# The last 224 rows of w_out as one row a lane: fewer pieces in the MLP, other DMA engines

## The chip, the cores and the metric

The kernel runs on one core of a Trainium2 chip. Its time is the device time of one execution in microseconds (us). The engines are PE (matrix products), DVE (VectorE), ACT (ScalarE), POOL (GpSimd) and SP, which here only issues transfers. The core's transfers run on sixteen DMA engines.

## What is computed

One decoding step for four sequences: the sum of the input, of attention with a key and value cache, and of a gated MLP, both on the normalised input.

```python
B, Sq, D = 4, 1, 640;  H = 32 heads, Sk = 4096 cached keys, Dh = 128;  F = 1728, Fh = 864
xn = layernorm(x)
q = xn @ wq                                        # 640 x 4096
p = softmax(q . k_cache * Dh ** -0.5)              # for each sequence and head
att = (p . v_cache) @ wo                           # 4096 x 640
z = gelu(xn @ w_in)                                # 640 x 1728, tanh form
g = w_sp * layernorm(z[Fh:]) + b_sp                # w_sp and b_sp are single numbers
out = x + att + (z[:Fh] * g) @ w_out               # 864 x 640
```

All tensors are bf16. The two caches have 134 MB each and are read once; the other weights together are some 14 MB.

## The kernel before

The attention is cut into 16 units, `NU`: a group of 8 heads (`HG` = 4 groups) of one sequence. A unit's keys are 8 MB, laid with 256 keys a lane on 128 lanes, in four tiles of 64 keys a lane; they live in seven places of `k_ring`. A unit's values are 8 MB and fill `v_all`. For each key tile DVE multiplies by the broadcast query (`product`, L537) and adds the halves (`fold_half`, L543), and PE sums the rest with identity products into PSUM (`sums`, L555). DVE then takes row sums (L569), the maximum (L578 to L588), ACT the exponentials (L596), DVE lays them out by head in `p_m` (L607), and PE multiplies by the values (`weighted`, L631). A group of four units ends with a projection by `wo` (L699).

The order on PE, DVE, ACT and SP is written out by hand: the loop over `NK * NU` = 64 key tiles at the end of the function. Transfers stand in the list `loads`; `pump()` issues from it on SP's queue, in order, as long as the places of the next entry are free. Each DMA also takes one of eight completion semaphores in turn and waits until that one's last user has landed.

At the start v_all isn't needed for values yet, so `wq`, `w_in` and most of `w_out` are put there. The 864 rows of `w_out` are cut by `W_OUT` into parts (lanes, rows a lane, transfers): 128 lanes of 5 rows in `v_all`; 128 lanes of 1 row in `p_m`; and 12 lanes of 8 rows in `p_m`, loaded as four transfers of every fourth lane, so of 3 lanes each with 8 rows of 640 bf16 (10240 bytes) a lane. The last part is `load_w_few`, behind the second half of unit 0's keys:

```python
loads = [k_load(0, 0, 1), k_load(0, 1, 2), (load_w, []), k_load(0, 2, 4), (load_w_few, []), k_load(1)]
```

The number of rows a lane over all parts, `NFC` = 5 + 1 + 8 = 14, is the number of pieces in which the MLP runs: `gmlp()` makes 2 x 14 x 5 products with `w_in` (L404), element steps on tiles of 128 x (2 x 14 x 4) (L414 to L432, L488 to L500) and 14 x 2 products with `w_out` (L503). It runs in steps between the first key tiles. The first values can be loaded when L503 is done with `v_all` (`busy.remove(V)`).

The input `x` (4 rows) is one transfer on ACT's queue (L101); the two single numbers `w_sp` and `b_sp` are loaded on the same queue just before the loop (L735, L736) and cast on POOL (L464, L466). The query path is x, its statistics and normalisation (L265 to L274), its transposition (L289, L294), and q (L303), which needs `wq`.

The end of the kernel is the last unit's values in falling sizes, the last part of `wo` in six transfers, the last projection (L699), one copy on ACT (L823) and two output transfers.

Of the kernel before, what the change touches and what calls it, by code (L numbers as in the profile page):

```python
# [10 lines left out]
BF16 = mybir.dt.bfloat16  # L11
# [6 lines left out]
def kernel(  # L18
# [14 lines left out]
    nc = tc.nc  # L33
    P = nc.NUM_PARTITIONS
    Bsz, Sq, D = A_x.shape
    _, H, S, Dh = A_k_cache.shape
    HD = A_wq.shape[1]
    F = B_w_in.shape[1]
    Fh = F // 2
# [19 lines left out]
    RW = 8  # L59
    QW = HC * Dh  # L60
    RING = 2 * NK - 1
    W_OUT = ((P, 5, 1), (P, 1, 1), (12, 8, 4))
    assert sum(n * r for n, r, _ in W_OUT) == Fh
    NFC = sum(r for _, r, _ in W_OUT)

    def up(n):
        return -(-n // 256) * 256

    PW = sum(up(r * D) for _, r, _ in W_OUT[1:])
    NOH = D // 2  # L70
    CB = 4
    NG = NR // CB
# [8 lines left out]
    const = ctx.enter_context(tc.tile_pool(name="const", bufs=1))  # L81
# [16 lines left out]

    ring = places.tile([P, RING, QW], BF16, name="k_ring")
    x_bf = ring[0:Bsz, 1, 0:D]  # L100
    nc.scalar.dma_start(out=x_bf, in_=A_x.flatten_outer_dims())  # L101
    v_all = places.tile([P, NK * QW], BF16, name="v_all")

    wq_sb = v_all[:, 0 : DC * HD].rearrange("p (c n) -> p c n", c=DC)
# [2 lines left out]

    at_v = up(DC * (HD + F))
    w_parts, f0, at_p = [], 0, 0
    for n, r, t in W_OUT:  # L110
        if f0 == 0:
            room = v_all[0:n, at_v : at_v + r * D]
        else:
            room = p_buf[0:n, at_p : at_p + r * D]
            at_p += up(r * D)
        w_parts.append((room.rearrange("p (k n) -> p k n", k=r), f0, n, r, t))
        f0 += n * r
    nc.sync.dma_start(out=wq_sb, in_=A_wq.rearrange("(p c) n -> p c n", c=DC))

    def load_part(part):  # L120
        w, f0, n, r, t = part
        rows = B_w_out[f0 : f0 + n * r].rearrange("(p k) n -> p k n", k=r)
        for l in range(t):
            nc.sync.dma_start(out=w[l:n:t], in_=rows[l:n:t])

    def load_w():
        nc.sync.dma_start(out=w_in_sb, in_=B_w_in.rearrange("(p c) n -> p c n", c=DC))
        for part in w_parts:
            if part[4] == 1:
                load_part(part)  # L130

    def load_w_few():
        for part in w_parts:
            if part[4] > 1:
                load_part(part)

    w_rows = [
        (w[:, i], f0 + i, n, r) for w, f0, n, r, _ in w_parts for i in range(r)
    ]

    def run_of(cache, u):
# [18 lines left out]
    def k_load(u, r0=0, r1=NK):  # L160
        at = k_at[u][r0:r1]

        def go():
            nc.sync.dma_start(
                out=ring[:, at[0] : at[0] + r1 - r0, :],
                in_=run_of(A_k_cache, u)[:, r0 * QW : r1 * QW].rearrange("p (r w) -> p r w", w=QW),
            )

        return go, at
# [22 lines left out]
    def wo_load(hg):  # L192
        return (lambda: load_wo(hg)), [WO_AT]

    loads = [k_load(0, 0, 1), k_load(0, 1, 2), (load_w, []), k_load(0, 2, 4), (load_w_few, []), k_load(1)]
    for u in range(NU - 4):
        loads += [v_load(u), k_load(u + 2)]
        if u % Bsz == Bsz - 1:
# [44 lines left out]
    for e in range(PAR):  # L243
        nc.gpsimd.tensor_copy(
            out=of_row[:, e, :, :, e, :],
            in_=ident[:].rearrange("p (k q) -> p q k", q=QD)[:, 0:Bsz, :, None].to_broadcast(
                [P, Bsz, NQ, LN]
            ),
# [15 lines left out]
    for i in range(NSTAT):  # L264
# [5 lines left out]
        out=rstd[:], in_=mv[:, 1:2], func=ACT.Sqrt, bias=eps_tile[:Bsz], scale=1.0  # L270
# [4 lines left out]
        out=xn_bf,  # L275
# [4 lines left out]
        op1=ALU.mult,  # L280
    )

    wsp_bf = const.tile([1, 1], BF16)
    bsp_bf = const.tile([1, 1], BF16)

    xn_v = xn_bf.rearrange("b (p c) -> b c p", c=DC)
    xnT_ps = ps_m.tile([P, DC, Bsz], BF16, tag="m")
    for c in range(DC):
        nc.tensor.transpose(  # L289
            out=xnT_ps[:, c, :], in_=xn_v[:, c, :], identity=ident[:Bsz, :Bsz]  # L290
# [8 lines left out]
    for e in range(PAR):  # L299
        q_ps = ps_pv.tile([P, HG, Dh], FP32, tag="pv", name="q_ps")  # L300
        for c in range(DC):
            for k in range(NQ):
                nc.tensor.matmul(  # L303
                    out=q_ps[k * QD : (k + 1) * QD],
# [5 lines left out]
        rows = const.tile([P, HG, Dh], BF16, name=f"q_rows{e}")  # L310
        nc.vector.tensor_scalar(  # L311
            out=rows[:], in0=q_ps[:], scalar1=scale_qk, scalar2=None, op0=ALU.mult
# [7 lines left out]
        out=hot[:].rearrange("p c h -> p (c h)"),  # L320
        in_=ident[:].rearrange("p (g m) -> p m g", m=QD),
# [6 lines left out]
        out=pick[:, :, Bsz - 1 :].rearrange("p c (k q) -> p c k q", q=QD)[  # L328
            :, :, :, 0 : PAR * Bsz : Bsz
        ],  # L330
        in_=hot[:].rearrange("p c (k e) -> p c k e", e=PAR),
# [4 lines left out]
        out=of_set[:],  # L336
        in_=hot[:].rearrange("p c h -> p (c h)")[:, 0 : PAR * Bsz].rearrange(
            "p (e b) -> p e b", b=Bsz
        ),
# [5 lines left out]
    with nc.allow_low_precision("0 and 1"):  # L345
        nc.vector.tensor_reduce(
            out=own[:],
            in_=ident[:].rearrange("p (h l) -> p h l", h=HT),
# [5 lines left out]
        out=par[:], in_=own[:].rearrange("p (k e) -> p e k", e=PAR), axis=AX.X, op=ALU.add  # L354
# [3 lines left out]
        out=far[:],  # L358
# [13 lines left out]
    for half in range(2):  # L372
        nc.tensor.matmul(
            out=out_ps[OG * half : OG * half + OG, :],
# [13 lines left out]
    gm["yT"] = work.tile([P, NFC, Bsz], BF16, name="yT")  # L388

    by_lanes = []  # L390
    for n, r, _ in W_OUT:
        if by_lanes and by_lanes[-1][0] == n:
            by_lanes[-1] = (n, by_lanes[-1][1] + r)
        else:
            by_lanes.append((n, r))
# [336 lines left out]
    E = mybir.EngineType  # L732
    with tc.manual_schedule(engines={E.PE, E.DVE, E.Activation, E.SP}):
        stage_q(0)
        nc.scalar.dma_start(out=wsp_bf[:], in_=B_w_sp[0:1, 0:1])  # L735
        nc.scalar.dma_start(out=bsp_bf[:], in_=B_b_sp[0:1].rearrange("(a b) -> a b", a=1))  # L736
        waiting = None
        mlp = gmlp()
        for n in range(NK * NU):
            u, i = divmod(n, NK)  # L740
            product(n)
            if n and n % 2 == 0:
                row_sums(n - 1)
            if i == 0 and u:
                head_max(u - 1)
                if waiting in taken:
                    picked(waiting)
            fold_half(n)
            if n == 1:
                next(mlp)  # L750
                next(mlp)
            if i == 0 and u:
                exps(u - 1)
                if waiting in pvs:
                    take(waiting)
                by_head(u - 1)
            sums(n)
            if i == 0 and u + 1 < NU:
                stage_q(u + 1)
            if i == 0 and waiting is not None:  # L760
                if waiting in taken:
                    picked(waiting)
                if waiting % Bsz == Bsz - 1:
                    group_turn(waiting // Bsz)
                    group_proj(waiting // Bsz)
                waiting = None
            if n == 0:
                next(mlp)
            if n == 1:
                next(mlp)  # L770
                next(mlp)
                next(mlp)
                busy.remove(V)
            if n in turns:
                w = waiting = turns[n]
                if w % Bsz == Bsz - 1:
                    group_den(w // Bsz)
                if w == NU - 3:
                    weighted(w, v_runs[:, 0:NC], more=True)
                    weighted(w, v_runs[:, NC:NR], NG // 2)  # L780
                else:
                    weighted(w, v_runs)
                if i < NK - 1:
                    take(w)
                busy.remove(V)
            pump()
        weighted(NU - 2, v_runs)
        row_sums(NK * NU - 1)
        head_max(NU - 1)
        exps(NU - 1)  # L790
        take(NU - 2)
        by_head(NU - 1)
        den = ps_m.tile([P, NQ, PAR, Bsz], FP32, tag="m", name="den_all")
        nc.tensor.matmul(
            out=den[:],
            lhsT=ones_sq[:],
            rhs=acc[(HG - 1) % NACC][:, :, 0 : PAR * Bsz],
            start=True,
            stop=True,
        )  # L800
        rden = small.tile([P, NQ, PAR, Bsz], FP32, name="rden_all")
        nc.vector.reciprocal(out=rden[:], in_=den[:])
        picked(NU - 2)
        u, b = NU - 1, Bsz - 1
        weighted(u, v_ends[0])
        take(u)
        pick_last(u, more=True)
        for c in range(NC):
            nc.tensor.matmul(  # L809
                out=o_last[0][:, :, :, b],  # L810
                lhsT=v_ends[1][:, c, :],
                rhs=p_m[:, u % 2, NG // 2 + c // CB, c % CB, :].rearrange("p (k e) -> p k e", e=PAR),
                start=False,
                stop=(c == NC - 1),
            )
        o_n = small.tile([P, NQ, PAR, Bsz], BF16, name="o_n_last")
        nc.vector.tensor_tensor(out=o_n[:], in0=o_last[0][:], in1=rden[:], op=ALU.mult)  # L817
        gr[HG - 1] = [o_n[:, h // PAR, h % PAR, :] for h in range(HT)]
        group_proj(HG - 1)

        res = v_all[:, 0:NOH]
        out_v = out.flatten_outer_dims()
        nc.scalar.copy(out=res[0 : OG + Bsz], in_=out_ps[0 : OG + Bsz])  # L823
        nc.scalar.dma_start(out=out_v[:, 0:NOH], in_=res[0:Bsz])
        nc.sync.dma_start(out=out_v[:, NOH:D], in_=res[OG : OG + Bsz])
# [30 lines left out]
```

## Time and profile before

| | us |
|---|---|
| median of 3 runs | 661.87 (661.77 to 662.01) |
| profiled execution, its time | 662.09 |
| span of the profile | 660.2 |
| DVE busy | 522.6 (79%) |
| PE busy | 317.0 (48%) |
| ACT busy | 29.9 (5%) |
| HBM read | 282.24 MB, 428 GB/s over the span |

The span begins with the first instruction and ends with the last; what lies around it is 1.9 us. Busy times of different engines overlap. "q1" is the queue that SP issues to, "q10" that of ACT, "q8" and "q14" fetch instructions. In a waits view each line says which instruction waited for which, the time in total, the count and the longest; "SPq" is SP's issuing of transfers. A timeline line has start, duration, engine, line, operation, output<-input, shapes and count. The trace also holds each DMA packet with its start, duration and size, but not the DMA engine that moved it.

### The profile page before, as it was taken

To read this page: it belongs to the slowest core of one execution; us is meant where nothing else is said; L and a number is where in the kernel's file an instruction comes from. 1 tells how busy PE (TensorE), PEld (TensorE's weight loads), DVE (VectorE), ACT (ScalarE), POOL (GpSimd) and SP (SyncE) were. 2 spreads that over 40 slices of the span, in tenths; PEclk is the share of its full clock that TensorE was granted. 3 is DMA by queue.
4 is the path that set the end of the run, shared out by engine and by line. 5 is a ranking of instruction groups with operands and counts; after the bars stand their busy time and mean duration, and the time that the engine had idled before them with its cause. 6 is when DMAs were issued, how large, how long until landed. Compare 5 with 4: busy or idle time off the path is not lost.

```text
span 660.2 us, 4777 instructions
## 1 busy us (share of the span) xinstructions
PE 317.0 (48%) x2083; PEld 136.3 (21%) x2083; DVE 522.6 (79%) x276; ACT 29.9 (5%) x73; POOL 10.1 (2%) x20
## 2 busy tenths in 40 slices
PE   0574372526427363452636336263452534737367
PEld 0231121212213121120212112121120211212124
DVE  1767978959597795969959598695969969999950
ACT  0020000000000000000000000000000000000000
POOL 2300000000000000000000000000000000000000
PEclk9757676766767676585767768676685867676785
DMA  9999999999999999999999999999999999999997
GB/s 369 433 461 434 417 441 434 433 437 438 421 445 426 437 430 441 437 422 433 434 441 441 418 437 441 430 441 421 434 441 437 426 421 445 422 427 436 449 409 284
DMA packets 8232, 282.55 MB, mean 428 GB/s; under 512 B 892, under 2 KB 2184, under 8 KB 2568
## 3 DMA queue, kind: packets, MB, share of 16 engines
q1 hardware_dynamic: 8192, 282.25, 99.1%
q8 instruction: 16, 0.26, 0.1%
q10 hardware_dynamic: 20, 0.01, 0.0%
q14 instruction: 4, 0.03, 0.0%
HBM read 282.24 MB, written 0.01 MB: 428 GB/s over the span
## 4 chain that ended last, share of the span: by engine, by line
DMA 62%; DVE 28%; PE 8%; issue 1%; ACT 0%; DVEq 0%
DMA k_ring<-in_A_k_cache_dram 53%; DVE k_ring L537 14%; DVE k_ring L543 7%; PE s_ps L555 6%; DMA v_all<-in_A_v_cache_dram 4%; DMA k_ring<-in_A_wo_dram 3%; DVE s_sb L569 3%; DMA v_all<-in_A_wq_dram 2%; DVE p_m L607 1%; DVE m L578 1%; PE q_ps L303 1%; PE pv L631 1%; PE out_ps L699 1%; DVE p_m L678 1%; DVE mf L580 1%
## 5 line engine op out<-in xcount | busy, mean ns | idle before, releaser
L537 DVE TENSOR_TENSOR k_ring<-k_ring,qbc 128x8192 bf16<-128x8192 bf16 x64 | 282.9, 4420 | 88.5 <-DMA k_ring<-in_A_k_cache_dram 87.9
L555 PE MATMUL s_ps<-k_ring,ident 128*128 128x512 bf16 x512 | 202.2, 566 | 313.8 <-DVE k_ring L543 313.7
L555 PEld LDWEIGHTS <-ident 128*128 128x128 bf16 x512 | 64.0, 130 | 430.0 <-issue 245.4
L543 DVE TENSOR_TENSOR k_ring<-k_ring 128x4096 bf16<-128x4096 bf16 x64 | 145.9, 2280 | 1.1
L631 PE MATMUL pv<-v_all,p_m 128*32 128x512 bf16 x960 | 62.5, 419 | 0.0
L569 DVE TENSOR_REDUCE s_sb<-s_ps 128x128 f32<-128x1024 f32 x32 | 39.0, 1218 | 3.7 <-PE s_ps L555 3.7
L607 DVE TENSOR_TENSOR p_m<-p_c,own 128x2048 bf16<-128x2048 bf16 x16 | 36.6, 2285 | 0.7 <-ACT p_c L596 0.7
L631 PEld LDWEIGHTS <-p_m 128*32 128x32 bf16 x992 | 26.6, 106 | 42.5 <-issue 23.3
L596 ACT ACTIVATE p_c<-s_sb,nm 128x256 bf16<-128x256 f32 x16 | 8.1, 508 | 342.9 <-DVE nm L588 342.9
L662 PEld LDWEIGHTS o_ps<-o_rows,pick 128*128 128x128 f32 x96 | 20.4, 294 | 4.3 <-issue 3.3
L662 PE MATMUL o_ps<-o_rows,pick 128*128 128x128 f32 x96 | 19.1, 367 | 0.0
L643 ACT COPY o_rows<-pv 128x512 f32<-128x512 f32 x16 | 9.4, 586 | 165.7 <-PE pv L631 165.7
L311 DVE TENSOR_SCALAR q_rows<-q_ps 128x512 bf16<-128x512 f32 x2 | 1.4, 692 | 12.8 <-PE q_ps L303 12.8
L817 DVE TENSOR_TENSOR o_n_last<-o_last,rden_all 128x32 bf16<-128x32 f32 x1 | 0.2, 192 | 12.2 <-PE o_last L809 12.2
L303 PE MATMUL q_ps<-v_all,xnT 128*32 128x512 bf16 x40 | 4.5, 630 | 9.3 <-DMA v_all<-in_A_wq_dram 9.3
L527 ACT CAST qbc<-qbc_ps 128x128 bf16<-128x128 f32 x16 | 4.3, 266 | 97.6 <-PE qbc_ps L519 97.6
L578 DVE TENSOR_REDUCE m<-s_sb 128x1 f32<-128x256 f32 x16 | 6.7, 420 | 0.5
L519 PE MATMUL qbc_ps<-q_rows,of_row 128*128 128x128 bf16 x32 | 6.0, 276 | 0.6 <-DVE q_rows L311 0.6
L519 PEld LDWEIGHTS <-of_row 128*128 128x128 bf16 x32 | 4.1, 132 | 8.1 <-issue 7.4
L716 PE MATMUL o_last<-hot,o_rows 128*128 128x8 f32 x32 | 4.9, 279 | 0.7 <-ACT o_rows L643 0.7
L716 PEld LDWEIGHTS o_last<-hot,o_rows 128*128 128x128 f32 x32 | 4.8, 226 | 1.8 <-ACT o_rows L643 1.6
L699 PE MATMUL out_ps<-k_ring,p_m 128*4 128x320 bf16 x48 | 4.0, 309 | 2.1 <-DVE p_m L691 2.1
(87 smaller groups left out, 81.4 us busy)
## 6 DMA issues: line engine op xcount, KB each, us to landing
k_ring<-in_A_k_cache_dram SPq DMA_DIRECT2D x5, 4096.0 KB, 27.2
v_all<-in_A_v_cache_dram SPq DMA_DIRECT2D x2, 4096.0 KB, 28.2
v_all<-in_A_wq_dram SPq DMA_DIRECT2D x1, 5120.0 KB, 15.4
k_ring<-in_A_k_cache_dram SPq DMA_DIRECT2D x2, 2048.0 KB
k_ring<-in_A_v_cache_dram SPq DMA_DIRECT2D x1, 4096.0 KB
k_ring<-in_A_wo_dram SPq DMA_DIRECT2D x3, 1280.0 KB, 20.6
v_all<-in_B_w_in_dram SPq DMA_DIRECT2D x1, 2160.0 KB
k_ring<-in_A_v_cache_dram SPq DMA_DIRECT2D x1, 2048.0 KB
```

Of the source, the lines that this page charges most:

```text
L303: nc.tensor.matmul(out=q_ps[k * QD : (k + 1) * QD], lhsT=xnT[:, c, :], rhs=wq_v[:, c, k, e], start=(c == 0), stop=(c == DC - 1),)
L519: nc.tensor.matmul(out=qb_ps[:], lhsT=of_row[:, e, b].rearrange("p k f l -> p (k f l)"), rhs=q_rows[e][:, hg, :], start=(e == 0), stop=(e ...
L537: nc.vector.tensor_tensor(out=t, in0=t, in1=qbcs[u][:, None, :].to_broadcast([P, HC, Dh]), op=ALU.mult)
L543: nc.vector.tensor_tensor(out=t[:, :, 0:HD2], in0=t[:, :, 0:HD2], in1=t[:, :, HD2:Dh], op=ALU.add)
L555: nc.tensor.matmul(out=s, lhsT=ident[:], rhs=t[:, :, g * RW : (g + 1) * RW], start=(g == 0), stop=(g == m - 1),)
L569: nc.vector.tensor_reduce(out=scores[u][:].rearrange("p (r c) -> p r c", r=NK)[:, lo : hi + 1 : hi - lo], in_=sums_ps.pop(n // 2)[:], axis ...
L578: nc.vector.tensor_reduce(out=m1[:], in_=scores[u][:], axis=AX.X, op=ALU.max)
L607: nc.vector.tensor_tensor(out=p_m[:, u % 2], in0=p_c.pop(u)[:].rearrange("p (g c) -> p g c", c=CB)[:, :, :, None].to_broadcast([P, NG, CB, HT]
L631: nc.tensor.matmul(out=pvs[u][cg * QD : (cg + 1) * QD, :], lhsT=p_m[:, u % 2, g0 + n].rearrange("p c h -> p (c h)"), rhs=v_at[:, n * CB : ...
L662: nc.tensor.matmul(out=gr[hg][:], lhsT=pick[:, c, Bsz - 1 - b : P + Bsz - 1 - b], rhs=o[:, c, :], start=(b == 0 and c == 0), stop=(b == Bs ...
L699: nc.tensor.matmul(out=out_sum(half), lhsT=o, rhs=wo_sb[:, n, half * NOH : (half + 1) * NOH], start=False, stop=(hg == HG - 1 and n == HT ...
L716: nc.tensor.matmul(out=o_last[0][:, :, :, u % Bsz], lhsT=o[:, c, :], rhs=hot[:, c, :].rearrange("p (k e) -> p k e", e=PAR), start=(c == 0) ...
```

## The change

The last 224 rows of `w_out` are laid one row a lane: a part of 103 lanes, loaded in transfers of 95, 5 and 3 lanes, and one of 121 lanes, loaded in transfers of 57 and 64 lanes. All five go ahead of the second half of unit 0's keys, and `load_w_few` is gone. The MLP then has 5 + 1 + 1 = 7 pieces. The buffer under `p_m` shrinks, since it no longer has to hold 8 rows a lane. `x` is loaded in two transfers of two rows, and `w_sp` and `b_sp` directly behind it, on ACT's queue. The new parameters `near` and `engine` have one value each here: every row is `near`, and no transfer is on POOL.

```diff
-    W_OUT = ((P, 5, 1), (P, 1, 1), (12, 8, 4))
+    W_OUT = (
+        (P, 5, True, (("wide", 0, 128, 1),)),
+        (103, 1, True, (("wide", 0, 95, 1), ("wide", 95, 5, 1), ("wide", 100, 3, 1))),
+        (121, 1, True, (("wide", 0, 57, 1), ("wide", 57, 64, 1))),
+    )
...
-    nc.scalar.dma_start(out=x_bf, in_=A_x.flatten_outer_dims())
+    x_rows = A_x.flatten_outer_dims()
+    for b0, b1 in ((0, 2), (2, 4)):
+        nc.scalar.dma_start(out=x_bf[b0:b1], in_=x_rows[b0:b1])
+    wsp_bf = const.tile([1, 1], BF16)
+    bsp_bf = const.tile([1, 1], BF16)
+    nc.scalar.dma_start(out=wsp_bf[:], in_=B_w_sp[0:1, 0:1])
+    nc.scalar.dma_start(out=bsp_bf[:], in_=B_b_sp[0:1].rearrange("(a b) -> a b", a=1))
...
     def load_part(part):
-        w, f0, n, r, t = part
-        rows = B_w_out[f0 : f0 + n * r].rearrange("(p k) n -> p k n", k=r)
-        for l in range(t):
-            nc.sync.dma_start(out=w[l:n:t], in_=rows[l:n:t])
+        w, f0, n, r, near, cuts = part
+        rows = B_w_out[f0 : f0 + n * r].rearrange(
+            "(p k) n -> p k n" if near else "(k p) n -> p k n", k=r
+        )
+        for engine, l, m, step in cuts:
+            end = l + (m - 1) * step + 1
+            dma = nc.gpsimd if engine == "pool" else nc.sync
+            dma.dma_start(out=w[l:end:step], in_=rows[l:end:step])

     def load_w():
         nc.sync.dma_start(out=w_in_sb, in_=B_w_in.rearrange("(p c) n -> p c n", c=DC))
         for part in w_parts:
-            if part[4] == 1:
-                load_part(part)
-
-    def load_w_few():
-        for part in w_parts:
-            if part[4] > 1:
-                load_part(part)
+            load_part(part)
...
-    loads = [k_load(0, 0, 1), k_load(0, 1, 2), (load_w, []), k_load(0, 2, 4), (load_w_few, []), k_load(1)]
+    loads = [k_load(0, 0, 1), k_load(0, 1, 2), (load_w, []), k_load(0, 2, 4), k_load(1)]
...
         stage_q(0)
-        nc.scalar.dma_start(out=wsp_bf[:], in_=B_w_sp[0:1, 0:1])
-        nc.scalar.dma_start(out=bsp_bf[:], in_=B_b_sp[0:1].rearrange("(a b) -> a b", a=1))
```

More of the change, by code (lines that the diff above doesn't have):

```diff
@@ L61 @@
     RING = 2 * NK - 1
-    W_OUT = ((P, 5, 1), (P, 1, 1), (12, 8, 4))
-    assert sum(n * r for n, r, _ in W_OUT) == Fh
-    NFC = sum(r for _, r, _ in W_OUT)
+    W_OUT = (
[3 more added lines that the diff above has]
+    )
+    assert sum(n * r for n, r, _, _ in W_OUT) == Fh
+    NFC = sum(r for _, r, _, _ in W_OUT)
     def up(n):
         return -(-n // 256) * 256
-    PW = sum(up(r * D) for _, r, _ in W_OUT[1:])
+    PW = sum(up(r * D) for _, r, _, _ in W_OUT[1:])
     NOH = D // 2
@@ L109 @@
     w_parts, f0, at_p = [], 0, 0
-    for n, r, t in W_OUT:
+    for n, r, near, cuts in W_OUT:
         if f0 == 0:
@@ L115 @@
             at_p += up(r * D)
-        w_parts.append((room.rearrange("p (k n) -> p k n", k=r), f0, n, r, t))
+        w_parts.append((room.rearrange("p (k n) -> p k n", k=r), f0, n, r, near, cuts))
         f0 += n * r
@@ L128, in load_w @@
         for part in w_parts:
-            if part[4] == 1:
-                load_part(part)
-    def load_w_few():
-        for part in w_parts:
-            if part[4] > 1:
-                load_part(part)
+            load_part(part)
     w_rows = [
-        (w[:, i], f0 + i, n, r) for w, f0, n, r, _ in w_parts for i in range(r)
+        (w[:, i], f0 + i * (1 if near else n), n, r if near else 1)
+        for w, f0, n, r, near, _ in w_parts
+        for i in range(r)
     ]
@@ L281 @@
     )
-    wsp_bf = const.tile([1, 1], BF16)
-    bsp_bf = const.tile([1, 1], BF16)
     xn_v = xn_bf.rearrange("b (p c) -> b c p", c=DC)
@@ L390 @@
     by_lanes = []
-    for n, r, _ in W_OUT:
+    for n, r, _, _ in W_OUT:
         if by_lanes and by_lanes[-1][0] == n:
```

## The prediction

> **What bounds the kernel now.** I read the page first (busy shares, slices, DMA queues), then the waits of VectorE (DVE), of SP, the chain at its end, and last the single DMA packets of the trace.
>
> ```profile
> span 660.2 us, 4777 instructions
> PE 317.0 (48%) x2083; PEld 136.3 (21%) x2083; DVE 522.6 (79%) x276; ACT 29.9 (5%) x73; POOL 10.1 (2%) x20
> DMA  9999999999999999999999999999999999999997
> q1 hardware_dynamic: 8192, 282.25, 99.1%
> q8 instruction: 16, 0.26, 0.1%
> ```
>
> No engine is full, but SP's DMA queue (q1) is busy 99.1% of sixteen engines' span, without an open slice until the last. The 16 packets of q8 are instruction fetches, 16 KB each; they matter below. DVE waits on keys:
>
> ```profile
> DVE k_ring L537 <- DMA k_ring<-in_A_k_cache_dram: 87.9, 13, 7.6
> DVE o_n_last L817 <- PE o_last L809: 12.2, 1, 12.2
> ```
>
> So compute follows the transfers, with 87.9 us to spare in 13 waits. SP waits too, but in order to issue, with work already queued (first 75 us, then the timeline there):
>
> ```profile
> SPq L164 <- DMA v_all<-in_A_wq_dram: 11.7, 1, 11.7
> SPq L175 <- PE out_ps L503: 13.3, 1, 13.3
> ```
>
> ```profile
> 16.12 0.33 SPq L164 DMA_DIRECT2D k_ring<-in_A_k_cache_dram  x1
> 31.96 4.61 PE L404 MATMUL zT<-xnT,v_all 128*128 128x4 bf16 x140
> 32.04 0.34 SPq L164 DMA_DIRECT2D k_ring<-in_A_k_cache_dram  x1
> 46.04 2.70 PE L503 MATMUL out_ps<-p_m,yT 128*4 128x320 bf16 x18
> ```
>
> The chain of waits in order of time ends so; the last matmul of L699 begins at 656.96, 0.04 after the last landing:
>
> ```profile
> 634.09 21.98 DMA k_ring<-in_A_wo_dram
> 656.07 0.04 issue
> 656.11 1.29 PE out_ps L699 x8
> 657.43 0.42 ACT v_all L823
> ```
>
> The single packets then say which DMA engine is last. On one engine a packet starts 4 ns before the one ahead ends, which strings them into sixteen chains. No chain has a hole, apart from fetches, from 1.7 us to its end: each engine simply works off its own list, and the longest list sets the time. A list's length has three sources. First, the start: the wq packets end between 14.54 and 15.76, because the first packet of each engine takes 1.5 to 2.8 us. Second, the fetches: q8's go round eight of the sixteen engines, two each, and each costs its engine 1.41 us (0.91 hole, 0.50 on the next 64 KB packet). Third, the 12-lane w_out part: its four 3-lane transfers put four 10240-byte packets on each of three engines; those three have no q8 fetch. The sum closes: when the last 16 KB packets end, the latest engine stands at 648.29 = 15.17 (its wq end) + 630.30 + 2 x 1.41; the others with two fetches at 647.66 to 647.99; the three with the few-lane packets at 646.62, 646.81 and 647.11; the five others at 645.09 to 646.63. What the change does to each group is the question.
>
> **The change, part by part.**
>
> *w_out's last 224 rows.* Prices, start to start, are from the same packets: 1280 bytes 51.7 ns, 10240 bytes 381 ns, the closing 4-byte packet 6 ns. Before, every engine has 8 x 51.7 + 6 = 420 ns for the 128-lane part, and the three engines 4 x 387 = 1548 more, 1968. After, how are 95, 5, 3, 57 and 64 lanes laid over engines? In the trace each engine that a transfer uses has the same share: 8 of 128 lanes, 1 of 3, 1 of x's 4. An equal share with at most 16 engines means 5 engines by 19 for 95, 3 by 19 for 57, 5 by 1, 3 by 1 and 16 by 4 for 64. Then three engines have 19 + 1 + 1 + 19 + 4 = 44 packets and five closings, 2305 ns: +337. Two have 24 and three closings, 1259: +839. Eleven have 4 and one, 213: -207. The other bound is an even spread, 6 of 95, 4 of 57, 1 each, 4: some 14 to 16 packets on most engines, about 0.35 us more than the 420. I take equal shares, since every size in the trace shows them.
>
> The two-fetch engines lose 0.207: the latest goes to 648.08. The three go to 647.45 at most, 0.63 short of it. The two with +839 come, at the latest of the five, to 646.88 if they are of the group without q8 fetches. That the three were, and that a 4-lane x used the neighbours, speaks for it; no packet names its engine. Sum: -0.21 us.
>
> The Trainium skill, "DMA: Bandwidth & Descriptors" ("Rules for kernel authors", Use all 16 engines), speaks against such lane counts: an outer size that is no multiple of 16 confines a transfer to fewer engines; that section's rule on k gives 5 for 95 lanes and 3 for 57, the lowest-numbered. The four-packet engines of the trace agree for 3 lanes. But the rule's harm falls here on engines 1.18 us or more ahead.
>
> *When they are issued.* The built programs use eight completion semaphores in turn, so a DMA waits for the eighth before it. The few-lane transfers move ahead of the second half of unit 0's keys, and that half waits for the second key tile instead of wq. Its packets end at 25.49; landing takes 0.4 (wq: 15.76, q_ps starts 16.15); issue at about 25.9 instead of 16.12, and first packet 1.0 later (wq: 0.73 to 1.74), 26.9. The fastest engine needs it at 31.32 + 0.21 = 31.53. Cost 0, hidden by w_in's and w_out's packets with 4.6 us to spare; without that cover each us late costs one. Behind it on SP stand unit 1's keys, still held by w_in's landing and PE to about 32.04, needed at 41.4. The 3-lane waits on w_sp and b_sp (7.95 us of issue in the timeline) vanish, into cover as well.
>
> *MLP in 7 pieces.* L404 goes from 140 matmuls to 70, half of 4.61 us; L503 from 28 to 14, half of 4.20; the DVE steps on 128x112 (L418 to L430, some 0.25 each) halve their width, and one copy of some 0.2 is added. That frees v_all earlier for the first values (SP's 13.3 us wait), which are queued behind 15 us of keys anyway. Gain 0; cover is the 87.9 us.
>
> *Fewer PE instructions.* The listing has 168 fewer of 3910 PE rows, so fetches fall later and the 16th (at 654.56) probably drops out. It is on an engine that isn't last: 0. Bounds: -0.2 if the latest engine were spared one (the next stands 0.2 behind), +0.
>
> *x in two transfers, w_sp and b_sp early.* Three more DMAs on ACT before the table load, 0.2 to 0.5 each; x perhaps 0.5 later, xnT at 7.6 instead of 7.1, and wq lands at 16.1: 0. They share the first microseconds with wq's first packets, so the start lottery may fall differently: the latest two-fetch engine lies 0.63 above the smallest and 0.59 below the largest start. Taken 0, bounds -0.6 to +0.6.
>
> *Addresses.* p_m is 1248 columns smaller, so qbc moves by a multiple of 32 bytes. L537's 64 runs are 4416 to 4427 ns, and qbc's place wasn't varied in them; taken 0.
>
> Against the profiled execution, 662.09 (span 660.2): 662.09 - 0.21 = 661.88. The median of the runs shown is 0.22 lower: 661.87 - 0.21 = 661.66, say 661.7. A difference under 0.2%, 1.32 us, is about what a measurement can tell from none.
>
> **The rivals.**
>
> *Confined engines last* (0.13). If the two with +839 are two-fetch engines: 661.87 + 0.84 = 662.7. If shares are even: 662.2. For it: nothing names engines or shows 95 lanes; against: equal shares.
>
> *Fetches hidden* (0.05). If fetches cost nothing at the end, the three engines would be last, and their +0.34 gives 662.2. The holes of 0.91 us speak against it. The Trainium skill, "Runtime: NRT & Kernel Launch" ("Instruction fetch mechanics"), calls crossing a 16 KiB boundary mostly hidden; for the engine that carries it the trace disagrees, 1.41 us.
>
> *Slower: dear small packets* (0.10). Packets of 1280 bytes were only seen with all engines writing. If 19 in a row on three to five engines cost twice as much, 103 ns, the three gain 44 x 51.7 = 2.27 more: 649.72 against 648.29 before, +1.43, 663.3. It passes the old end from 19 ns dearer on, (648.29 - 647.45)/44. Against: one line, 8 ns and 27.2 bytes a ns, fits every size from 1280 (55 ns) to 65536 bytes (2418 ns), whoever else writes.
>
> *Slower: a starved queue or a slower L537* (0.04). Keys over 4.6 us later than reckoned, or products over 1.4 us longer (5.5 us of DVE slack in a unit's 38.7, four products): 664 and beyond.
>
> *Faster* (0.08). A kinder start and one fetch less give 661.87 - 0.21 - 0.6 - 0.2 = 660.9; under 660.55 something must go that the packets do not show.
>
> **How the numbers follow.** The forecast has 0.60: 661.7, by the start bounds 661.1 to 662.3. Confined engines and hidden fetches lie within 0.2% too: same 0.60 + 0.13 + 0.05 = 0.78. Faster 0.08, slower 0.10 + 0.04 = 0.14. The range takes nearly all of the lucky start, 660.7, and reaches to 663.3, which holds the confined engines with an unlucky start and ends at the dear packets; what lies outside is 0.04 above and some 0.06 below.
>
> **What would show it.** Right: two groups of engines with 44 and 24 packets of 1280 bytes, q1 without a hole at 27 to 42 us, 15 or 16 fetches, the latest engine still one with two, L404 x70 near 2.3 us. Wrong: holes near 31 us, 1280-byte packets well over 55 ns, L537 off 4.42 us, or a last landing more than 1.3 us from 656.9.

## The result and the profile after

The changed kernel takes 663.06 us (median of 22 runs, 662.80 to 670.12); the kernel before took 661.92 beside it (22 runs, 661.76 to 662.23). The ratio of the means is 1.0045, with an interval of 1.003 to 1.006: slower, by less than half a percent but clear of 1. (All ratios below are of means too, each to the kernel before, run beside it.) The forecast was 661.7 and no measurable change.

The median hides what happened. Of the 22 times, 14 lie at 662.80 to 663.72 and 8 at 667.58 to 670.12, with nothing between; taken once more, the change gave 4 low and 8 high. So there are two sizes to explain: about +1 us in every run, and some 5 us more in 16 of 34. The kernel before never passed 662.5 in 107 runs.

The page of after, from a run of the low kind (time 662.80; before's profiled execution had 662.09):

```profile
span 660.8 us, 4614 instructions
PE 311.1 (47%) x1999; PEld 133.5 (20%) x1999; DVE 522.3 (79%) x277; ACT 29.7 (4%) x73; POOL 4.3 (1%) x20
DMA  8999999999999999999999999999999999999997
q1 hardware_dynamic: 8280, 282.25, 99.1%
q8 instruction: 15, 0.25, 0.1%
```

Fewer PE instructions, one fetch less and a queue as full as before, 99.1%, with no open slice: by these lines nothing is lost. The lines of after stand 8 below those of before from the value loads on (L537 is now L545). Its waits, of DVE over the whole span and of SP in the first 75 us:

```profile
DVE k_ring L545 <- DMA k_ring<-in_A_k_cache_dram: 89.6, 14, 8.4
DVE o_n_last L823 <- PE o_last L815: 13.1, 1, 13.1
```

```profile
SPq L185 <- PE out_ps L511: 11.2, 1, 11.2
SPq L174 <- DMA v_all<-in_B_w_in_dram: 4.8, 1, 4.8
SPq L174 <- DMA k_ring<-in_A_k_cache_dram: 4.2, 1, 4.2
```

DVE waits on keys 1.7 us more, as it does when keys come later. The timeline of the start:

```profile
7.86 0.87 DVE L275 BATCH_NORM_STATS2 stats<-k_ring 4x6 f32<-4x320 bf16 x2 [7.86 <-DMA k_ring<-in_A_x_dram]
16.46 3.73 PE L311 MATMUL q_ps<-v_all,xnT 128*32 128x512 bf16 x40 [4.76 <-DMA v_all<-in_A_wq_dram]
26.11 6.19 SPq L174 DMA_DIRECT2D k_ring<-in_A_k_cache_dram  x2
31.93 4.01 PE L412 MATMUL zT<-xnT,v_all 128*128 128x4 bf16 x70
```

x lands at 7.86 where it landed at 3.01 before, yet q_ps still starts on wq, at 16.46. The second key half is issued at 26.11 (I had said 25.9). And the chain of waits at its end, every step 0.63 later than before:

```profile
634.72 21.98 DMA k_ring<-in_A_wo_dram
656.70 0.04 issue
656.74 1.29 PE out_ps L707 x8
```

Where the time goes shows only when the same stretches of the kernels are set side by side. In the windows view each line is a stretch: its bounds and length, busy time of PE, PEld, DVE, ACT and POOL, the granted clock, the DMA engines' busy share and, last, the GB/s they moved. First the kernel before, then the changed one in its low run, then in a high one (time 668.78):

```profile
30.00:36.00 6.00, 6.00 (x131) 4.77 (x130) 5.33 (x2) 1.55 (x2) 3.08 (x1) 0.78 1.12 474
36.00:78.00 42.00, 19.77 (x89) 7.21 (x87) 33.07 (x32) 4.19 (x8) 0.00 (x0) 0.61 1.02 439
84.00:640.00 556.00, 267.91 (x1617) 111.83 (x1616) 464.65 (x224) 21.17 (x58) 0.00 (x0) 0.69 1.00 433
```

```profile
30.00:36.00 6.00, 5.93 (x77) 4.72 (x75) 4.92 (x2) 1.55 (x2) 0.00 (x0) 0.50 1.09 396
36.00:78.00 42.00, 16.55 (x52) 5.82 (x53) 31.64 (x33) 4.14 (x8) 0.00 (x0) 0.55 1.02 439
84.00:640.00 556.00, 267.67 (x1620) 111.47 (x1618) 466.11 (x224) 20.58 (x57) 0.00 (x0) 0.69 1.00 433
```

```profile
30.00:36.00 6.00, 5.63 (x76) 4.59 (x74) 4.88 (x5) 1.55 (x2) 0.00 (x0) 0.50 1.11 384
36.00:78.00 42.00, 14.15 (x44) 4.83 (x45) 27.14 (x31) 3.88 (x7) 0.00 (x0) 0.58 1.02 385
84.00:640.00 556.00, 261.70 (x1555) 108.85 (x1555) 466.74 (x220) 19.95 (x55) 0.00 (x0) 0.69 1.00 433
```

The DMA engines are busy throughout (1.0 and above), but what they move falls. From 30 to 36 us, where the five small transfers run, it is 474 GB/s before and 396 after. In the high run the lower rate stays: 385 instead of 439 until 78 us, and from 84 us on all three are at 433.

The single packets give the sizes. Against the line of size and duration in the prediction, the packets of 30 to 36 us take 0.85 us an engine too long in the low run (0.00 before): the sum of what they take beyond that line, divided by sixteen. Only 0.13 of it is in the 1280-byte packets themselves (median 58 ns, longest 96, where all took 55); 0.70 is in the 32 KB key packets that are moved meanwhile, up to 1744 ns instead of 1213. Strung into chains as in the prediction, all sixteen engines lose alike, 0.74 to 0.90 us each. In the high run every 64 KB packet of every engine takes 2784 to 2793 ns instead of 2418 until 80.5 us, then 2418 again.

### The profile page after: what moved, and what is told of

The parts are those of the page before. It is cut to its first block, busy times and chain, and to the rows that moved or that the text cites. A ratio compares the mean times of both kernels' runs of the same rounds, so it can differ in the third digit from the quotient of the medians.

```text
span 660.8 us, 4614 instructions
## 1 busy us (share of the span) xinstructions
PE 311.1 (47%) x1999; PEld 133.5 (20%) x1999; DVE 522.3 (79%) x277; ACT 29.7 (4%) x73; POOL 4.3 (1%) x20
## 3 DMA queue, kind: packets, MB, share of 16 engines
q1 hardware_dynamic: 8280, 282.25, 99.1%
## 4 chain that ended last, share of the span: by engine, by line
DMA 62%; DVE 28%; PE 8%; issue 1%; ACT 0%; DVEq 0%
DMA k_ring<-in_A_k_cache_dram 53%; DVE k_ring L545 14%; DVE k_ring L551 7%; PE s_ps L563 6%; DMA v_all<-in_A_v_cache_dram 4%; DMA k_ring<-in_A_wo_dram 3%; DVE s_sb L577 3%; DMA v_all<-in_A_wq_dram 2%; DVE p_m L615 1%; DVE m L586 1%; PE out_ps L707 1%; PE pv L639 1%; DVE p_m L686 1%; PE q_ps L311 1%; DVE mf L588 1%
## 5 line engine op out<-in xcount | busy, mean ns | idle before, releaser
L545 DVE TENSOR_TENSOR k_ring<-k_ring,qbc 128x8192 bf16<-128x8192 bf16 x64 | 282.9, 4420 | 90.2 <-DMA k_ring<-in_A_k_cache_dram 89.6
L815 PE MATMUL o_last<-p_m,k_ring 128*128 128x8 bf16 x128 | 4.0, 172 | 1.4 <-DMA k_ring<-in_A_v_cache_dram 1.4
```

Of the source, the lines that this page charges most:

```text
L545: nc.vector.tensor_tensor(out=t, in0=t, in1=qbcs[u][:, None, :].to_broadcast([P, HC, Dh]), op=ALU.mult)
```

## The experiments

Three groups of causes were tried: first x or the start (X, S, L), then the order of the small transfers and the keys (O), and the small packets, either by the unequal shares of the engines (Q) or by the lanes they write (P). For P, the map of lanes comes from the Trainium skill, "DMA: Bandwidth & Descriptors", "The descriptor swizzle": in a 128-lane transfer each engine writes two groups of four neighbouring lanes, so lanes 0 to 3 are one engine's, 4 to 7 the next one's, up to lane 31. The 12-lane part before, cut at every fourth lane, then has each engine on lanes of its own; a cut of 95 or 57 neighbours, 19 an engine, has not. No trace names an engine or a lane, so the runs had to decide.

**The change once more** (after_again).

> The changed kernel once more, for its spread. So far 14 of 22 runs lie at 662.8 to 663.7 and 8 at 667.6 to 670.1. Theory X (the second x transfer): it comes behind wq's packets on ACT's queue, x is complete at 7.9 us instead of 3.0, in some runs later still; a profile of a 667 run would show DVE waiting for x far longer than 7.9 and q after 16.5. Theory S (w_sp and b_sp): the 57-lane transfer waits for b_sp's semaphore, and unit 0's second key half stands behind it; a 667 run would show a hole of about 5 us in q1 near 31 us, x as before. Theory L (start): nothing but the first packets' delay; a 667 run would show one wq packet ending some 5 us late. All: both clusters again.

667.51 (12 runs, 662.78 to 669.95), ratio 1.0069 (1.0046 to 1.0092). Its profile is the last of the three windows fences above: x as late as in the low run, no hole in q1, and slow packets instead. No wq packet is late either: the last ends at 15.28. What differs between the two kinds of run is the packets' rate, above all from 34 to 80 us, not the start. S and L fall by this profile.

**x in one transfer, the rest as changed** (x_one).

```diff
-    for b0, b1 in ((0, 2), (2, 4)):
-        nc.scalar.dma_start(out=x_bf[b0:b1], in_=x_rows[b0:b1])
+    nc.scalar.dma_start(out=x_bf, in_=x_rows)
```

> The change with x in one transfer, w_sp and b_sp still early. Theory X: x lands near 3.0 us, no run above 664, median 661.6 to 662.0. Theory S: the 667s stay, in about a third of the runs, low cluster 662 to 663. Theory L: low cluster anywhere from 661.2 to 662.8, 667s stay.

665.31 (12 runs), 6 at 662.51 to 663.30 and 6 at 667.32 to 669.83; ratio 1.0052 (1.0029 to 1.0074). DVE's wait shows that x is early again, and both kinds of run remain:

```profile
DVE stats L274 <- DMA k_ring<-in_A_x_dram: 2.7, 1, 2.7
```

**The kernel before with x in two transfers** (before_x_two), **and with w_sp and b_sp early** (before_sp_early). The edits are those of the change, alone; first the one, then the other:

```diff
-    nc.scalar.dma_start(out=x_bf, in_=A_x.flatten_outer_dims())
+    x_rows = A_x.flatten_outer_dims()
+    for b0, b1 in ((0, 2), (2, 4)):
+        nc.scalar.dma_start(out=x_bf[b0:b1], in_=x_rows[b0:b1])
```

```diff
     nc.scalar.dma_start(out=x_bf, in_=A_x.flatten_outer_dims())
+    wsp_bf = const.tile([1, 1], BF16)
+    bsp_bf = const.tile([1, 1], BF16)
+    nc.scalar.dma_start(out=wsp_bf[:], in_=B_w_sp[0:1, 0:1])
+    nc.scalar.dma_start(out=bsp_bf[:], in_=B_b_sp[0:1].rearrange("(a b) -> a b", a=1))
...
         stage_q(0)
-        nc.scalar.dma_start(out=wsp_bf[:], in_=B_w_sp[0:1, 0:1])
-        nc.scalar.dma_start(out=bsp_bf[:], in_=B_b_sp[0:1].rearrange("(a b) -> a b", a=1))
```

> The kernel before with x in two transfers and nothing else. Theory X: x lands near 7.9 us, median 662.5 to 663, some runs at 667 and above. Theory S: no 667s, since the keys are issued ahead of what waits for b_sp; 661.7 to 662.8. Theory L: 661.2 to 662.8 by the start alone.

> The kernel before with w_sp and b_sp issued right behind x, and nothing else. All theories: 661.7 to 662.1 without 667s; X says so since x is one transfer, S since the second key half is ahead of the waits. A run at 667 would speak for the two small transfers themselves disturbing the start.

661.88 and 661.89 (11 runs each), ratios 0.9999 (0.9991 to 1.0008) and 1.0000 (0.9991 to 1.0009). Both edits cost nothing, though x lands at 7.7 us in before_x_two. X, which had forecast 662.5 to 663 there and no high run in x_one, falls too. What is left is w_out. For the high runs that is argued: every kernel that showed them also loads w_sp and b_sp early and runs the MLP in 7 pieces, and no run took these away.

**The kernel before, its 3-lane transfers on neighbouring lanes** (few_side_by_side).

```diff
-            nc.sync.dma_start(out=w[l:n:t], in_=rows[l:n:t])
+            m = n // t
+            nc.sync.dma_start(out=w[l * m : (l + 1) * m], in_=rows[l * m : (l + 1) * m])
```

> The kernel before; its four 3-lane transfers take lanes next to each other (0 to 2, 3 to 5, ...) instead of every fourth lane; same engines, sizes, order and counts. Theory P (lanes): an engine that writes lanes which another engine writes in a 128-lane transfer gets in its way. Then 10240-byte packets well over 385 ns and key packets over their 2418 ns from 41.6 us on, median 662.2 or more, perhaps runs at 666 and above. Theory Q (uneven lists): what disturbs is that few engines have much and the others go ahead to the keys; nothing changes here, 661.8 to 662.0. The Trainium skill, DMA: Bandwidth & Descriptors (The descriptor swizzle), gives in a 128-lane transfer engine 0 the lanes 0 to 3 and 32 to 35, engine 1 the next four, and so on; by that every fourth lane keeps three engines on their own lanes.

662.11 (11 runs), ratio 1.0002 (0.9993 to 1.0011): too little for the times to tell, and the median is just under P's 662.2. The packets do tell: the twelve of 10240 bytes, all 385 ns before, now have a quarter over 567 and one of 776, and the packets of 40 to 46 us are 0.14 us an engine too long, 0.00 before. Only the three engines that move them lose, 0.5 to 0.9 us each; of the others one key packet is 79 ns late.

**Equal shares, neighbouring lanes** (ninety_six): the last 224 rows as 128 and 96 lanes, so 14 packets on each engine.

```diff
-        (103, 1, True, (("wide", 0, 95, 1), ("wide", 95, 5, 1), ("wide", 100, 3, 1))),
-        (121, 1, True, (("wide", 0, 57, 1), ("wide", 57, 64, 1))),
+        (P, 1, True, (("wide", 0, 128, 1),)),
+        (96, 1, True, (("wide", 0, 96, 1),)),
```

> The change with the last 224 rows as 128 lanes and 96 lanes, one transfer each, still 7 pieces and ahead of the keys. Sixteen equal shares, but the 96 lanes are cut six to an engine, so mostly on lanes of other engines. Theory P: 1280-byte packets over 55 ns and slow key packets from 31.5 us on, though only 96 packets; 662.3 to 663, perhaps some runs at 667. Theory Q: all packets 55 ns, no run over 663; each engine has 14 packets instead of 8, +0.31, so 662.2.

662.52 (12 runs, two of them at 667.20 and 667.93), ratio 1.0021 (1.0005 to 1.0037). Excess at 30 to 36 us: 0.18 us an engine, nearly all in one key packet on each. Less of both, but equal shares remove neither, which speaks against Q.

**The small transfers behind the second key half** (keys_first).

```diff
-        for part in w_parts:
-            load_part(part)
+        load_part(w_parts[0])
+
+    def load_w_few():
+        for part in w_parts[1:]:
+            load_part(part)
...
-    loads = [k_load(0, 0, 1), k_load(0, 1, 2), (load_w, []), k_load(0, 2, 4), k_load(1)]
+    loads = [k_load(0, 0, 1), k_load(0, 1, 2), (load_w, []), k_load(0, 2, 4), (load_w_few, []), k_load(1)]
```

> The change with its five transfers behind the second half of unit 0's keys, where the 3-lane ones were; all else as in the change. Theory O (order): the trouble comes from the small packets meeting the 32 KB key packets, or from the keys issued late; then 661.7 to 662.2 and no run over 664. Theories P and Q: the same trouble, now near 41 to 45 us with unit 1's 64 KB packets; 662.5 to 663.3 and part of the runs at 667 and above.

664.61 (12 runs), 6 at 662.58 to 662.88 and 6 at 666.34 to 668.61; ratio 1.0048 (1.0027 to 1.0069). The profile is of a high run (666.36), and its windows show the loss moved along with the transfers, which are now at 40 us:

```profile
30.00:36.00 6.00, 5.24 (x78) 3.75 (x76) 5.79 (x7) 1.55 (x2) 0.00 (x0) 0.95 1.05 452
40.00:46.00 6.00, 4.13 (x20) 1.42 (x18) 2.75 (x5) 1.45 (x2) 0.00 (x0) 0.50 1.13 397
84.00:640.00 556.00, 266.53 (x1564) 110.12 (x1567) 465.08 (x221) 20.14 (x55) 0.00 (x0) 0.68 1.00 433
```

The packets have no excess before 40 us (0.03 at a fetch); then 64 KB take 2714 ns (median) until 78.08 us. O falls: the slow stretch begins where the small transfers are, whatever stands behind them.

**32 lanes of 7 rows, at every fourth lane** (thirty_two): the kernel before with eight lanes in each of four transfers, each engine on its own lanes by the map.

```diff
-    W_OUT = ((P, 5, 1), (P, 1, 1), (12, 8, 4))
+    W_OUT = ((P, 5, 1), (32, 7, 4))
```

> The kernel before with its last 224 rows as 32 lanes of 7 rows, four transfers of 8 lanes, every fourth lane (0, 4, ... 28 and so on), behind the keys as before; 12 pieces. Theory P: eight engines each write their own lanes, 28 rows each, the others none: packets at their line (8960 bytes 337 ns), no runs over 663, and the engines with two instruction fetches lose their 0.42 us of the 128-lane part: 661.4 to 661.6, provided the eight are those without such fetches. Theory Q: lists more uneven than before (1.37 against 0 us), so slow packets near 41 us and 662.5 or more.

662.97 (11 runs, 662.74 to 663.57; before beside it 661.92), ratio 1.0016 (1.0007 to 1.0025). P is right on the packets: all 32 of 8960 bytes take 338 ns, with no excess beside them. Its time is wrong. Eight engines now carry 0.95 us more, and the chains show the 0.91 us holes of q8 fetches in three of the eight; 661.92 + 0.95 = 662.87. That is the step that "confined engines last" priced.

**The same on neighbouring lanes** (thirty_two_side): the edit of few_side_by_side and nothing else, so the same eight engines, bytes and order.

> thirty_two (32 lanes of 7 rows in four transfers of 8 lanes, median 662.97, all packets of 8960 bytes at 338 ns) with one thing changed: each transfer takes 8 lanes side by side (0 to 7, 8 to 15, ...) instead of every fourth. Engines, packets, sizes, order and issues are the same. Theory P (lanes of other engines): 8960-byte packets far over 338 ns, key packets of 64 KB over 2418 ns from 41 us on, median 663.5 or more, and runs at 667 and above as in the change, since 28 KB times eight go to lanes of few engines. Theory Q (uneven lists, 1.37 against 0 us, are what disturbs): as thirty_two, 662.7 to 663.2.

664.63 (5 runs, 664.20 to 664.80; before beside it 661.97), ratio 1.0038 (1.0024 to 1.0051): 1.66 us from this edit alone; its lowest run is above thirty_two's highest. The runs at 667 that P had also forecast did not come in these five. From 40 to 46 us, thirty_two and then this one:

```profile
40.00:46.00 6.00, 4.26 (x12) 1.44 (x12) 2.68 (x15) 2.36 (x4) 0.00 (x0) 0.62 1.11 479
```

```profile
40.00:46.00 6.00, 4.53 (x12) 1.65 (x12) 2.43 (x13) 2.09 (x4) 0.00 (x0) 0.50 1.17 348
```

479 GB/s become 348 with the DMA engines as busy. The 8960-byte packets go from 338 ns to a median of 752 (longest 1034), and key packets of 64 KB beside them reach 4532: 2.12 us an engine too long, of which only 0.69 is in the small packets. So which lanes the small transfers take decides whether there is a loss of the first size.

How the loss comes about is not settled, and P's reason, engines in each other's lanes, is too narrow. Strung into chains, the eight engines with w_out packets lose 2.07 to 2.27 us each, and the eight without any lose 1.88 to 2.12, six of them in a single key packet of 4519 to 4532 ns. If the eight wrote their own lanes in thirty_two, as P has it, lanes 0 to 31 are theirs, and the other eight write none of them in the key tiles. They were slowed as much. Also, the edit changes with the lanes which rows of `w_out` an engine reads at a time, and no run separates the two. The 64-lane transfer of the next run speaks against the reading, since by the map each engine reads four neighbouring rows there, as in a 128-lane transfer of one row a lane, which shows no excess.

**Five engines** (twenty): the kernel before with 64 lanes of 1 row and 20 lanes of 8.

```diff
-    W_OUT = ((P, 5, 1), (P, 1, 1), (12, 8, 4))
+    W_OUT = ((P, 5, 1), (64, 1, 1), (20, 8, 4))
```

> The kernel before with its last 224 rows as 64 lanes of one row (one transfer, four lanes to an engine) and 20 lanes of 8 rows (four transfers of 5 lanes, every fourth lane). Still 14 pieces and the order of before. The five engines get 1.55 us of large packets, all others only 4 rows instead of 8. If thirty_two's +1.05 came from engines with two instruction fetches among its eight (8 of them +0.95), and the first five have none, as the chains of the change show: -0.21 from the 64 lanes, +0.05 at most for the 32 packets of them that go to other engines' lanes: 661.7 to 661.8, no run over 663. If thirty_two was slower for its pieces or its packets themselves: 662.3 or more.

662.18 (11 runs; before beside it 661.97), ratio 1.0004 (0.9995 to 1.0013): above the 661.7 to 661.8 expected, and under the 662.3 of the other reading; the interval holds no difference too. The twenty packets of 10240 bytes all take 385 ns, on their own lanes. The 64-lane transfer, half of it on other engines' lanes by the map, costs 0.20 us an engine at 30 to 34 us, on all sixteen, which is what four packets fewer on each engine had saved. The five engines' chains hold no q8 fetch.

## Why the prediction was wrong

*What bounds the kernel.* Right. The sixteen lists set the end, and the last chain is after's as it was before's.

*The shares.* Right: 44 packets of 1280 bytes on three engines, 24 on two, 4 on eleven, and the five have no q8 fetch. With the old prices the two-fetch engines' lists are shorter by the 0.21 us I had reckoned. One sum was off: the two with 24 packets come, at the latest of the five, to 646.63 + 0.84 = 647.47, not 646.88; that is still 0.61 under the latest engine and changes nothing.

*The step that failed* is the price in the term for w_out's last rows: "1280 bytes 51.7 ns, 10240 bytes 381 ns", taken over for other lanes, with the reason "whoever else writes". Apart from x's four packets, every transfer behind that line is one that by the map leaves each engine on lanes of its own; that was hardly varied. The term is not -0.21 but -0.21 + 0.85 = +0.64 us (0.85 is the mean of the sixteen engines), and between the profiled executions of low runs the whole change is 662.80 - 662.09 = +0.71. The medians give +0.98 (662.90 for the 14 low runs, 661.92 before). Most of the 0.85, 0.70, fell on packets that the sum never listed: the keys beside the small transfers, on every engine.

*The dear packets.* I had this rival at 0.10, with another cause and place: few engines writing, on the three engines with 44 packets, at 103 ns each. The 1280-byte packets reached 96 ns, but their median was 58; the time was lost by the key packets beside them, and also where all engines write alike (ninety_six).

*Five microseconds more in 16 of 34 runs.* In no step or rival. In the high run 46 us (34 to 80) with each packet 15% longer cost 6.12 - 0.16 = 5.96 us an engine beyond the line, high against low; the times differ by 668.78 - 662.80 = 5.98. It was seen in after, x_one, keys_first and ninety_six, the kernels whose last 224 rows lie one a lane (and that also have the early w_sp and b_sp and the 7 pieces), and in none of the 167 runs of the kernel before, its two small edits, few_side_by_side, thirty_two, thirty_two_side and twenty (only 5 of them thirty_two_side's). In both high profiles it ended with one 8 KB fetch of q14: at 80.49 us in one, at 78.08 in the other; the low run has that fetch too, at 74.43. Why it sets in only in part of the runs, what keeps it up and why it ends there stays open; that the fetch ends it is argued from two coincidences.

*The later issue of the keys*, priced 0 with 4.6 us of cover: right, no hole in q1, and in keys_first, where the keys went first, the loss stayed.

*The MLP.* The price of 0 is right, a reason was wrong. L412 takes 4.01 us for 70 products, not 2.3: the granted clock from 30 to 36 us was 0.50, against 0.78 before, and at the same 0.50 ninety_six took 3.17, so the clock is not all of it. SP's wait for L511 fell from 13.3 to 11.2, behind queued keys, as said.

*x, w_sp and b_sp.* Priced 0, right, by before_x_two and before_sp_early. x landed at 7.86, not 0.5 later: the packets of its second transfer and of w_sp and b_sp came some 1.5 us apart on each engine, the time of one 40 KB packet of wq. wq's landing still came last.

*Addresses.* L545 took 4420 ns, as before: 0, right. *Fetches:* 15, as said.

*The range* of 660.7 to 663.3 holds the median of 663.06, by luck: the median is one of the 14 low runs, and the 8 high ones lie more than 4 us above the range.

## What to carry to other kernels

Cut a load of few lanes at every fourth lane (here up to eight lanes a transfer), so that by the map each DMA engine writes lanes that it also writes in the 128-lane transfers around it; the same bytes on neighbouring lanes cost 1.66 us. A queue that is 99% busy says nothing of its rate: read GB/s and packet durations by stretch, and charge a new transfer with what it does to the packets beside it. When times fall in two groups, take a profile of each before explaining the median.

## What the hardware showed that I had not expected

- A small transfer on neighbouring lanes can slow all sixteen engines alike, also those that have no part in it: in thirty_two_side each lost about 2.1 us, the eight without w_out packets mostly in one key packet, up to 4532 ns instead of 2418. With three engines (few_side_by_side) only the three lost.
- A short disturbance can leave all sixteen engines slower long after it has passed: 2789 ns for 64 KB instead of 2418, from 34 to 80 us.
- At the start of the kernel a second queue got one packet through for each 40 KB packet of the first: w_sp's and b_sp's packets of 2 and 4 bytes started 1.5 us apart (8.93, 10.44, 11.96 and 13.47 us).

None of the kernels tried is measurably faster than the kernel before.
